# A spectral layer followed by a feed-forward layer on one core: three chunks side by side in the first feed-forward pass, a weight conversion in five stages without GpSimd, and batch 1 behind that pass

## The chip, the cores and the metric

The kernel runs on one core of one Trainium2 chip. The metric is the device time of one execution in microseconds (us), and lower is better. TensorE is called PE here, VectorE DVE, ScalarE ACT, GpSimd POOL; SP is the engine that issues all the transfers.

## The reference

Eight batches of 3008 x 256 numbers go through a spectral layer, and its output, 24064 rows of 256, through a feed-forward layer with 2048 hidden units. The two weights of the feed-forward layer are stored as 64-bit floats.

```python
X = np.fft.rfft(x, axis=1)
Yr = Xr @ w_r - Xi @ w_i + b_r
Yi = Xr @ w_i + Xi @ w_r + b_i
Yr = np.sign(Yr) * np.maximum(np.abs(Yr) - lam, 0.0)     # Yi likewise, lam = 0.01
y = np.fft.irfft(Yr + 1j * Yi, n=3008, axis=1)
h = y.reshape(24064, 256) @ w_in
out = (h - np.tanh(h)) @ w_out
```

## The kernel before

The Fourier transform of length 3008 = 64 x 47 is made of matrix products in stages, with the intermediate results kept in device memory. `Forward(b, ch)` makes the 47-point stage of batch b for four pairs of rows (eight `ch` for each batch, two halves `q` in each) and stores it to `a`. `Spectrum(b, jp)` (twelve `jp` for each batch; `WholeSpectrum` for batch 0) loads `at` from `a`, makes the 64-point stage (`dft`), the product with the complex weights (`cross`, `shared`), the thresholding (`shrink`, `join`) and the first stage back (`inverse`, `put`), and stores it to `z`. A `Chunk` is 5 pairs, 470 columns: it loads `zin` from `z` (which waits for all twelve stores of the batch), makes the last stage back (`time`) into `yh` and `yl`, the rounded part and the rest of the number, and then for each of the 16 blocks f of hidden units `up(f)` (6 matmuls into `h`; ACT makes the tanh `th`, DVE the difference `g`, ACT its rounded copy `gh`, DVE the rest `gl`) and `down(f)` (6 matmuls into two accumulators `o`). A matmul in this way is three products of rounded and rest parts.

`order` lists the pairs (chunk, f) of all FFN work. At step g the program issues `up` for step g + 2 and `down` for step g. The first pass takes chunks 0 and 1 in turn (32 steps), after that one chunk follows the other, 16 steps each. Transforms of later batches and the weight conversion are put into numbered slots, which `run(g)` issues at step g.

The head of the program, up to the first `time` of chunks 0 and 1, stands under `manual_schedule`: there each engine takes its instructions in the order in which the code is written. Everything behind it is ordered by the compiling layer's scheduler. Each engine works through its own list in order and waits at the first instruction whose inputs are not there. `idle(n)` issues n matmuls of 512 columns whose result nobody reads.

The weights come as 16 raw blocks of 512 KB, four for each quarter of f; `split_f64` turns one into two F32R tiles with integer operations: 6 on DVE, 3 on ACT and 2 on POOL for each block. Six blocks are converted in the head, ten in the first pass. Two chunks of the forward stage of batch 1 are made in the head (`following`), the other six from slot 8 on, the spectrum of batch 1 from slot 31 on, one unit every 4 steps.

## Time and profile before

| | before |
|---|---|
| median of 3 runs | 2720.86 us (2720.68 to 2721.68) |
| the profiled execution | 2719.45 us |
| its span, first to last instruction | 2717.2 us |
| PE busy | 2682.9 us, 99% of the span |
| DVE, ACT, POOL busy | 1746.0, 1388.9, 48.9 us |
| mean granted clock of PE | 0.996 of full speed |

The span is 2.3 us shorter than the execution that it was taken from, and that execution 1.4 us shorter than the median of the runs. Matmuls are pipelined, so two that follow each other overlap in the profile, and the time from one start to the next says more than the duration of one.

### The profile page before, as it was taken

What the parts mean: (1) busy time and instruction counts of PE and PEld (TensorE: products, weight loads), DVE (VectorE), ACT (ScalarE), POOL (GpSimd) and SP (SyncE); (2) the same over time, 40 slices, a digit from 0 to 9 for tenths busy, and PEclk for the clock granted to TensorE, in tenths of its full rate; (3) what the DMA queues carried; (4) which work ended last, traced back from release to release, by engine and by line L of the source; (5) the groups of instructions that cost most, each with busy time, mean ns of one, the idle gap of its engine ahead of it and who ended that gap; (6) DMA issues with size and microseconds to landing.
All of it is one profiled execution on the core that took longest, in us unless ns stands there. A gap on an engine that the chain in (4) does not pass through costs nothing.

```text
span 2717.2 us, 36997 instructions
## 1 busy us (share of the span) xinstructions
PE 2682.9 (99%) x14159; PEld 2390.0 (88%) x14159; DVE 1746.0 (64%) x3056; ACT 1388.9 (51%) x2606; POOL 48.9 (2%) x39
## 2 busy tenths in 40 slices
PE   8889999999999999999999999999999999999999
PEld 6679888999889998899988999899988999998989
DVE  5796775766656666567665666656675667655555
ACT  5664455444554445545455454645446544444445
POOL 1230000000000000000000000000000000000000
PEclk9899999999999999999999999999999999999999
DMA  6442114111141113211023110311104111100000
GB/s 198 146 127 65 47 52 125 42 49 36 36 115 49 38 36 96 75 46 49 28 58 101 38 53 30 105 58 48 49 23 123 46 42 40 35 22 22 20 19 17
DMA packets 105137, 163.49 MB, mean 60 GB/s; under 512 B 7488, under 2 KB 70976, under 8 KB 104864
## 3 DMA queue, kind: packets, MB, share of 16 engines
...
q14 instruction: 66, 0.54, 0.1%
...
## 4 chain that ended last, share of the span: by engine, by line
PE 92%; DVE 5%; ACT 2%; issue 1%; DMA 1%; POOL 0%; SPq 0%; DVEq 0%; ACTq 0%
PE o L437 36%; PE h L416 36%; PE ps_v L286 4%; PE ps_i L403 4%; PE ps_f L266 3%; PE ps_t L286 2%; DVE y L311 1%; PE ps_f L217 1%; PE ps_f L219 1%; PE ps_f L218 1%; PE ps_i L322 1%; PE ps_i L323 1%; PE ps_i L321 1%; DVE g L421 1%; DVE gl L425 0%
## 5 line engine op out<-in xcount | busy, mean ns | idle before, releaser
L421 DVE TENSOR_TENSOR g<-h,th 128x470 f32<-128x470 f32 (+1 forms) x832 | 532.0, 639 | 554.6 <-ACT th L419 547.0
L419 ACT ACTIVATE th<-h 128x470 f32<-128x470 f32 (+1 forms) x832 | 464.1, 558 | 765.9 <-PE h L416 765.6
L425 DVE TENSOR_TENSOR gl<-g,gh 128x470 fp32r<-128x470 f32 (+1 forms) x832 | 534.5, 643 | 289.3 <-ACT gh L423 204.8
L423 ACT CAST gh<-g 128x470 fp32r<-128x470 f32 (+1 forms) x832 | 483.1, 581 | 392.6 <-DVE g L421 384.3
L437 PE MATMUL o<-gh,wout_l 128*128 128x470 f32 (+1 forms) x1664 | 632.8, 380 | 0.1
L437 PE MATMUL o<-gl,wout_h 128*128 128x470 f32 (+1 forms) x1664 | 617.1, 371 | 3.1 <-DVE gl L425 3.1
L437 PE MATMUL o<-gh,wout_h 128*128 128x470 f32 (+1 forms) x1664 | 616.1, 370 | 0.0
L416 PE MATMUL h<-yh,win_l 128*128 128x470 f32 (+1 forms) x1664 | 481.0, 370 | 4.1 <-DVE g L421 4.1
L416 PE MATMUL h<-yl,win_h 128*128 128x470 f32 (+1 forms) x1664 | 481.1, 370 | 1.6 <-DVE yl L408 1.5
L416 PE MATMUL h<-yh,win_h 128*128 128x470 f32 (+1 forms) x1664 | 480.1, 369 | 0.0
L437 PEld LDWEIGHTS o<-gl,wout_h 128*128 128x128 f32 x1664 | 313.1, 188 | 44.8 <-DVE gl L425 6.2
L416 PEld LDWEIGHTS h<-yh,win_l 128*128 128x128 f32 x1664 | 310.6, 188 | 41.9 <-DVE g L421 5.1
L437 PEld LDWEIGHTS o<-gh,wout_l 128*128 128x128 f32 x1664 | 313.4, 188 | 35.2 <-DVE ot L446 1.3
L416 PEld LDWEIGHTS h<-yl,win_h 128*128 128x128 f32 x1664 | 310.7, 188 | 37.7 <-DVE yl L408 2.2
L437 PEld LDWEIGHTS o<-gh,wout_h 128*128 128x128 f32 x1664 | 313.9, 189 | 32.2
L416 PEld LDWEIGHTS h<-yh,win_h 128*128 128x128 f32 x1664 | 310.7, 188 | 35.6
L311 DVE TENSOR_TENSOR y<-tb,ps_v 64x256 f32<-64x256 f32 x384 | 160.0, 417 | 9.7 <-ACT tb L358 5.7
L403 PEld LDWEIGHTS ps_i<-i,zin 96*128 96x128 f32 x1024 | 126.2, 192 | 3.0
L403 PE MATMUL ps_i<-i,zin 96*128 96x94 f32 x1024 | 127.7, 272 | 0.0
L91 DVE TENSOR_TENSOR x_l<-xt,x_h 94x512 fp32r<-94x512 f32 x128 | 87.8, 694 | 54.1 <-ACT x_h L90 54.1
L266 PEld LDWEIGHTS ps_f<-f,at 128*128 128x128 f32 x768 | 99.5, 189 | 9.3 <-issue 4.3
L266 PE MATMUL ps_f<-f,at 128*128 128x128 f32 x768 | 101.1, 273 | 1.8 <-DMA at<-a 1.8
...
## 6 DMA issues: line engine op xcount, KB each, us to landing
...
w_raw<-in_moe_w_in SPq DMA_DIRECT2D x8, 512.0 KB, 4.2
w_raw<-in_moe_w_out SPq DMA_DIRECT2D x8, 512.0 KB, 4.4
```

The source lines that it names most:

```text
L91: rest.tensor_tensor(out=lo, in0=src, in1=hi.bitcast(F32), op=ALU.subtract)
L217: nc.tensor.matmul(pv, f1h, xl, start=True, stop=False)
L266: nc.tensor.matmul(pv[:, t, jj], self.at[:, jj, t * P:(t + 1) * P], rhs, start=True, stop=True)
L286: nc.tensor.matmul(dst, lhs[:, t], rhs[:, t, :], start=n == 0, stop=n == 5)
L311: nc.vector.tensor_tensor(out=y[ri * 64:(ri + 1) * 64, jj, :], in0=common(jj, ri), in1=self.vv[jj * 64:(jj + 1) * 64, ri * D:(ri + 1) * D] ...
L403: nc.tensor.matmul(ps[:, k * 94:(k + 1) * 94], self.zt[:, k, t * P:(t + 1) * P], i2t[:, p * 94:(p + 1) * 94], start=True, stop=True,)
L416: nc.tensor.matmul(h[:, :n], lhs[:, t, f * P:(f + 1) * P], rhs[:, t, :n], start=k == 0, stop=k == 5)
L419: nc.scalar.activation(out=th[:, :n], in_=h[:, :n], func=AF.Tanh)
L421: nc.vector.tensor_tensor(out=g[:, :n], in0=h[:, :n], in1=th[:, :n], op=ALU.subtract)
L423: nc.scalar.copy(out=gh[:, :n], in_=g[:, :n])
L425: nc.vector.tensor_tensor(out=gl[:, :n], in0=g[:, :n], in1=gh[:, :n].bitcast(F32), op=ALU.subtract)
L437: nc.tensor.matmul(self.o[t][:, :n], lhs[:, f, t * P:(t + 1) * P], rhs[:, :n], start=f == 0 and k == 0, stop=f == NF - 1 and k == 2,)
```

## The change

The program of each raw block is now five stages: `fields` (2 operations on DVE), `mantissa` (1 on ACT, 1 on DVE), `scale` (3 on DVE), `high` (1 on ACT), `low_part` (1 on DVE); POOL does none. `some(n)` issues the next n stages, taken in turn from two blocks that are under way. Six blocks are loaded in the loop of the head, two behind the loads of the chunks, eight in the first pass. The first pass runs chunks 0, 1 and 2 side by side (48 steps, chunk 0 two blocks f ahead), chunks 0 and 1 accumulate in the four `ps_f` banks and chunk 2 in the two `ps_o` banks, and steps up to 39 stand under `manual_schedule` too. `up` ends with `gh`; `gl` is made by `rest`, behind what `between` issues. The two chunks of batch 1's forward stage leave the head; all eight stand at slots 46 to 53, both halves of one in a slot, and its spectrum from slot 59 on, one unit every 2 steps. `idle` of 12 before the first `time` becomes 26, and one of 8 stands before the last `inverse` of batch 0. The three splits of the linear weights move from units 3 to 5 of the loop to units 0 to 2, and the loads of `at` run two units ahead instead of three.

```diff
-        def exponent():
+        def fields():
             nc.vector.tensor_scalar(out=s, in0=top, scalar1=20, scalar2=0x7FF, op0=ALU.logical_shift_right, op1=ALU.bitwise_and)
-            nc.vector.tensor_scalar(out=s, in0=s, scalar1=-896.0, scalar2=0.0, op0=ALU.add, op1=ALU.max)
+            nc.vector.tensor_scalar(out=m, in0=top, scalar1=0xFFFFF, scalar2=0x100000, op0=ALU.bitwise_and, op1=ALU.bitwise_or)
 
         def mantissa():
-            nc.vector.tensor_scalar(out=m, in0=top, scalar1=0xFFFFF, scalar2=0x100000, op0=ALU.bitwise_and, op1=ALU.bitwise_or)
-            nc.vector.tensor_scalar(out=s, in0=s, scalar1=254.0, scalar2=2.0**23, op0=ALU.min, op1=ALU.mult)
-            nc.scalar.mul(out=w, in_=low, mul=2.0**-32)
-            nc.scalar.copy(out=m.bitcast(F32), in_=m)
-            nc.gpsimd.tensor_tensor(out=w, in0=w, in1=m.bitcast(F32), op=ALU.add)
+            nc.scalar.activation(out=s.bitcast(F32), in_=s, func=AF.Relu, bias=rebias)
+            nc.vector.scalar_tensor_tensor(out=w, in0=low, scalar=2.0**-32, in1=m, op0=ALU.mult, op1=ALU.add)
 
         def scale():
+            nc.vector.tensor_scalar(out=s, in0=s.bitcast(F32), scalar1=254.0, scalar2=2.0**23, op0=ALU.min, op1=ALU.mult)
             nc.vector.scalar_tensor_tensor(out=s, in0=top, scalar=0x80000000, in1=s, op0=ALU.bitwise_and, op1=ALU.bitwise_or)
-
-        def parts():
             nc.vector.scalar_tensor_tensor(out=w, in0=w, scalar=2.0**-20, in1=s.bitcast(F32), op0=ALU.mult, op1=ALU.mult)
+
+        def high():
             nc.scalar.copy(out=hi_out, in_=w)
-            nc.gpsimd.tensor_tensor(out=lo_out, in0=w, in1=hi_out.bitcast(F32), op=ALU.subtract)
-
-        return exponent, mantissa, scale, parts
-
-    def ffn_weights(part, k):
-        for op in split_f64(part, k, load_f64(part, k, load, "zin")):
-            op()
-
-    def convert(units):
-        units = [split_f64(*u) for u in units]
-        ops = []
-        for i in range(len(units) + 1):
-            ops += units[i][:3] if i < len(units) else ()
-            ops += units[i - 1][3:] if i else ()
-        return ops
+
+        def low_part():
+            nc.vector.tensor_tensor(out=lo_out, in0=w, in1=hi_out.bitcast(F32), op=ALU.subtract)
+
+        return [fields, mantissa, scale, high, low_part]
...
+    FIRST = 3
...
-                self.yh = work.tile([P, 2, 512], F32R, name="yh", tag="yh")
-                self.yl = work.tile([P, 2, 512], F32R, name="yl", tag="yl")
+                tags = ("st", "st") if self.c == FIRST - 1 else ("yh", "yl")
+                self.yh, self.yl = (work.tile([P, 2, 512], F32R, name=m, tag=g) for m, g in zip(("yh", "yl"), tags))
...
             gh = ffn.tile([P, CT], F32R, name="gh", tag="g_h")
             nc.scalar.copy(out=gh[:, :n], in_=g[:, :n])
+            return g, gh
+
+        def rest(self, g, gh):
+            n = self.n
...
-                if self.c == 1:
+                if self.c < FIRST - 1:
...
-    order = [(g % 2, g // 2) for g in range(2 * NF)]
-    order += [(c, f) for c in range(2, NCH) for f in range(NF)]
+    SKEW = 2
+    order = [(0, f) for f in range(SKEW)]
+    for f in range(NF):
+        order += [(c, f) for c in range(1, FIRST)] + [(0, f + SKEW)] * (f + SKEW < NF)
+    order += [(c, f) for c in range(FIRST, NCH) for f in range(NF)]
...
-        where = {0: "yh", 1: "yl", 2: "yh", 3: "yl", 7: "yh", 8: "yl"}
-        raws, ops = [], []
...
+        homes = [(work, "yh"), (work, "yl")] * 2 + [(load, "xt")] * 6 + [(load, "zin")] * 2 + [(load, "xt")] * 2 + [(load, "zin")] * 2
+        streams = [[], []]
+        raw_count = 0
+        turn = 0
+
+        def load_raw(n):
+            nonlocal raw_count
+            for _ in range(n):
+                k = raw_count
+                raw_count += 1
+                raw = load_f64(k // 4, k % 4, *homes[k])
+                streams[k % 2].append((k, raw))
+
+        pending = [[], []]
+
+        def some(n):
+            nonlocal turn
+            for _ in range(n):
+                for side in (turn, 1 - turn):
+                    if not pending[side] and streams[side]:
+                        k, raw = streams[side].pop(0)
+                        pending[side] = split_f64(k // 4, k % 4, raw)
+                    if pending[side]:
+                        pending[side].pop(0)()
+                        turn = 1 - side
+                        break
...
+        raw_at = {0: 2, 4: 1, 5: 1, 9: 1, 10: 1}
+        some_at = (0, 2, 2, 1, 1, 1, 1, 2, 1, 2, 1, 2, 1)
+        for u in units[:2]:
+            u.load()
...
+            some(some_at[i])
+            if i == NU:
+                unit(i - 1).common()
...
+            if i < 3:
+                lin.append(split(whole_lin[i], f"w{i + 1}"))
...
-        u9, u10, u11 = units[-3:]
-        for q in range(2):
-            following[0].split(q)
+        u10, u11 = units[-2:]
         u10.inverse()
-        u11.common()
         u11.shrink()
-        for q in range(2):
-            following[0].dft(q)
         u10.put(u10.pz)
+        some(1)
         u11.join()
+        idle(8)
         u11.inverse()
         u11.put(u11.pz)
-        for c in range(2):
+        for c in range(FIRST):
             chunks[c].load()
-        for q in range(2):
-            following[0].keep(q)
-        for q in range(2):
-            following[1].split(q)
-        for op in ops[:6]:
-            op()
-        for q in range(2):
-            following[1].dft(q)
-            following[1].keep(q)
-        idle(12)
+        load_raw(2)
+        some(6)
+        idle(26)
         for c in range(2):
             for t in range(2):
                 chunks[c].time(t)
-            for op in ops[6 + c:7 + c]:
-                op()
-
-    for i in range(2):
-        put(2 * i - 2, ffn_weights, 1, 2 + i)
-    for i in range(8):
-        put(1 + 8 * i // 3, ffn_weights, 2 + i // 4, i % 4)
-    plan_forward(1, 8, 2, 3, LOOK)
-    plan_spectrum(1, 31, 4, 7, 2)
+        some(5)
+
+        ready, half = {}, {}
+
+        def step(g, between):
+            if g + AHEAD < len(order):
+                c, f = order[g + AHEAD]
+                half[g + AHEAD] = chunks[c].up(f)
+            between()
+            if g + AHEAD in half:
+                c, f = order[g + AHEAD]
+                ready[g + AHEAD] = chunks[c].rest(*half.pop(g + AHEAD))
+            if g < 0:
+                return
+            c, f = order[g]
+            chunks[c].down(f, *ready.pop(g))
+            if f == NF - 1:
+                chunks[c].store()
+
+        HELD = 40
+        raw_slots = (-1, 2, 6, 9, 13, 16, 19, 22)
+
+        def early(g):
+            if g == -1:
+                for t in range(2):
+                    chunks[2].time(t)
+            if g in raw_slots:
+                load_raw(1)
+            some(1 + (g % 5 in (0, 2)))
+
+        for g in range(-AHEAD, HELD):
+            step(g, lambda: early(g))
+    plan_forward(1, 46, 1, 3)
+    plan_spectrum(1, 59, 2, 3, 1)
...
-    for c in range(2, NCH):
+    for c in range(FIRST, NCH):
         at = NF * (c - 1)
-        put(at + {2: 9, 6: 6}.get(c, 2), chunks[c].load)
+        put(at + {FIRST: 8, 6: 7}.get(c, 2), chunks[c].load)
         for t in range(2):
-            put(at + (13 if c == 2 else 8 + 2 * t + (2 if c == 6 else 0)), chunks[c].time, t)
-    ready = {}
-    for g in range(-AHEAD, len(order)):
-        if g + AHEAD < len(order):
-            c, f = order[g + AHEAD]
-            ready[g + AHEAD] = chunks[c].up(f)
-        run(g)
-        if g < 0:
-            continue
-        c, f = order[g]
-        chunks[c].down(f, *ready.pop(g))
-        if f == NF - 1:
-            chunks[c].store()
+            put(at + (12 if c == FIRST else 10 + t if c == 6 else 8 + 2 * t), chunks[c].time, t)
...
+    for g in range(HELD, len(order)):
+        step(g, lambda: run(g))```

**DVE at the start of the first pass.** Before, from the last `yl` of chunk 0 on (`w_s`, `w_m`, `w_f` belong to the conversion):

```order
L161 TENSOR_SCALAR w_s<-w_raw 128x512
L165 TENSOR_SCALAR w_m<-w_raw 128x512
L162 TENSOR_SCALAR w_s<-w_s 128x512
L408 TENSOR_TENSOR yl<-ps_i_1015,yh 128x470
L408 TENSOR_TENSOR yl<-ps_i_1023,yh 128x470
L175 SCALAR_TENSOR_TENSOR w_f<-w_f,w_s 128x512
L421 TENSOR_TENSOR g<-h,th 128x470
L166 TENSOR_SCALAR w_s<-w_s 128x512
L421 TENSOR_TENSOR g<-h,th 128x470
L425 TENSOR_TENSOR gl<-g,gh 128x470
```

The same place after the change (L398 is `yl`, L411 `g`, L419 `gl`, L169 to L171 `scale`, L177 `low_part`):

```order
L398 TENSOR_TENSOR yl<-ps_i_990,yh 128x470
L169 TENSOR_SCALAR w_s<-w_s 128x512
L170 SCALAR_TENSOR_TENSOR w_s<-w_raw,w_s 128x512
L171 SCALAR_TENSOR_TENSOR w_f<-w_f,w_s 128x512
L169 TENSOR_SCALAR w_s<-w_s 128x512
L170 SCALAR_TENSOR_TENSOR w_s<-w_raw,w_s 128x512
L171 SCALAR_TENSOR_TENSOR w_f<-w_f,w_s 128x512
L177 TENSOR_TENSOR win_l<-w_f,win_h 128x512
L411 TENSOR_TENSOR g<-h,th 128x470
L177 TENSOR_TENSOR win_l<-w_f,win_h 128x512
L419 TENSOR_TENSOR gl<-g,gh 128x470
```

Seven operations of the conversion now stand between the last `yl` of chunk 1 and the first `g`, and conversion work stands between `g` and `gl` instead of behind `gl`.

**PE at the end of the head.** Before, from the inverse of unit 9 of batch 0 on (L217 to L219 are batch 1's forward stage, the last `ps_i` is unit 11):

```order
L373 MATMUL ps_i_892<-mn,i_f 128x512
L373 MATMUL ps_i_905<-mn,i_f 128x512
L217 MATMUL ps_f_918<-x_0_0_l,f_h 96x512
L218 MATMUL ps_f_918<-x_0_0_h,f_l 96x512
L219 MATMUL ps_f_918<-x_0_0_h,f_h 96x512
L217 MATMUL ps_f_922<-x_0_1_l,f_h 96x512
L218 MATMUL ps_f_922<-x_0_1_h,f_l 96x512
L219 MATMUL ps_f_922<-x_0_1_h,f_h 96x512
L373 MATMUL ps_i_930<-mn,i_f 128x512
L217 MATMUL ps_f_967<-x_1_0_l,f_h 96x512
```

After:

```order
L361 MATMUL ps_i_874<-mn,i_f 128x512
L361 MATMUL ps_i_879<-mn,i_f 128x512
L493 MATMUL idle<-warm 128x512 x8
L361 MATMUL ps_i_904<-mn,i_f 128x512
L493 MATMUL idle<-warm 128x512 x26
L393 MATMUL ps_i_964<-i_382,zin 128x94 x5
```

The forward stage of batch 1 is gone from here, and idle matmuls stand in its place on both sides of the last inverse.

**PE in the spectrum of batch 1.** Before, one FFN step with its filling (L286 is `cross` and `shared`, L416 `up`, L437 `down`):

```order
L416 MATMUL h<-yl,win_h 128x470 x2
L286 MATMUL ps_v<-w_h,xl 128x256 x2
L286 MATMUL ps_v<-w_l,xh 128x256 x2
L286 MATMUL ps_v<-w_h,xh 128x256 x2
L437 MATMUL o_2099<-gh,wout_l 128x470
```

After (L406 is `up`, L309 to L311 `inverse`, L274 `cross` and `shared`, L431 `down`):

```order
L406 MATMUL h<-yl,win_h 128x470 x2
L309 MATMUL ps_i_3205<-z_3_l,i_h 128x512
L310 MATMUL ps_i_3205<-z_3_h,i_l 128x512
L311 MATMUL ps_i_3205<-z_3_h,i_h 128x512
L274 MATMUL ps_t_3212<-w_h,s_4_l 128x256 x2
L274 MATMUL ps_t_3212<-w_l,s_4_h 128x256 x2
L274 MATMUL ps_t_3212<-w_h,s_4_h 128x256 x2
L274 MATMUL ps_v<-w_h,xl 128x256 x2
L274 MATMUL ps_v<-w_l,xh 128x256 x2
L274 MATMUL ps_v<-w_h,xh 128x256 x2
L431 MATMUL o_2934<-gh,wout_l 128x470
```

One step now carries work of three units (an inverse, a shared product, a cross product) between `up` and `down`.

## Rows read from the trace of the kernel before

**Rows 1.** The page, part 1: busy time, share of the span, instructions.

```profile
PE 2682.9 (99%) x14159; PEld 2390.0 (88%) x14159; DVE 1746.0 (64%) x3056; ACT 1388.9 (51%) x2606; POOL 48.9 (2%) x39
```

**Rows 2.** Windows by stage: length, busy of each engine (x), PEclk, DMA share, GB/s.

```profile
34.50:87.30 52.80, 49.03 (x234) 38.30 (x235) 36.40 (x75) 30.31 (x57) 11.69 (x9) 1.00 0.54 170
87.30:115.50 28.20, 20.07 (x67) 12.61 (x66) 18.35 (x37) 15.84 (x31) 4.11 (x3) 0.82 0.44 132
115.50:195.00 79.50, 69.71 (x321) 56.41 (x320) 73.81 (x117) 51.44 (x96) 31.44 (x23) 0.98 0.41 121
195.00:440.00 245.00, 243.97 (x1310) 214.27 (x1309) 170.19 (x303) 131.67 (x251) 0.20 (x1) 1.00 0.26 79
440.00:2717.00 2277.00, 2272.45 (x12142) 2049.81 (x12140) 1430.21 (x2495) 1142.64 (x2143) 0.00 (x0) 1.00 0.17 50
```

**Rows 3.** Timeline of PE in the head: start, duration, instruction, idle time before it.

```profile
60.23 0.46 PE L348 MATMUL ps_v<-brow,ones 33*128 33x512 f32 x1 [0.60 <-DVE y L311]
...
67.27 0.47 PE L348 MATMUL ps_v<-brow,ones 33*128 33x512 f32 x1 [2.04 <-DVE y L311]
...
73.18 0.46 PE L348 MATMUL ps_v<-brow,ones 33*128 33x512 f32 x1 [0.90 <-DVE y L311]
...
82.24 1.05 PE L266 MATMUL ps_f<-f,at 128*128 128x128 f32 x8
...
87.35 1.05 PE L266 MATMUL ps_f<-f,at 128*128 128x128 f32 x8
```

**Rows 4.** Timeline from unit 11's thresholding to the first chunk.

```profile
100.66 1.72 DVE L311 TENSOR_TENSOR y<-tb,ps_v 64x256 f32<-64x256 f32 x4
...
103.77 0.69 DVE L369 TENSOR_TENSOR mn<-up,mn 128x512 f32<-128x512 f32 x1 [1.40 <-ACT mn L365]
...
104.52 2.08 PE L373 MATMUL ps_i<-mn,i_f 128*128 128x512 f32 x2 [2.75 <-DVE mn L369]
...
115.54 4.60 PE L403 MATMUL ps_i<-i,zin 96*128 96x94 f32 x40
```

**Rows 5.** Waits of PE in 115.5 to 195: total us, times, longest.

```profile
PE h L416 <- DVE g L421: 4.1, 4, 1.5
PE o L437 <- DVE gl L425: 3.1, 5, 1.4
PE h L416 <- DVE yl L408: 1.5, 1, 1.5
PE ps_f L217 <- DVE x_l L91: 1.0, 1, 1.0
```

**Rows 6.** Timeline of DVE, pairs that follow each other without a wait.

```profile
112.55 0.68 DVE L172 SCALAR_TENSOR_TENSOR w_s<-w_raw,w_s 128x512 uint32<-128x512 uint32 x1
...
113.15 0.42 DVE L161 TENSOR_SCALAR w_s<-w_raw 128x512 uint32<-128x512 uint32 x1
...
122.41 0.42 DVE L165 TENSOR_SCALAR w_m<-w_raw 128x512 uint32<-128x512 uint32 x1
122.75 0.42 DVE L162 TENSOR_SCALAR w_s<-w_s 128x512 uint32<-128x512 uint32 x1
...
132.54 0.63 DVE L421 TENSOR_TENSOR g<-h,th 128x470 f32<-128x470 f32 x1
...
133.10 0.63 DVE L425 TENSOR_TENSOR gl<-g,gh 128x470 fp32r<-128x470 f32 x1
```

**Rows 7.** Groups of DVE in 115.5 to 195: busy, mean ns, idle before.

```profile
L425 DVE TENSOR_TENSOR gl<-g,gh 128x470 fp32r<-128x470 f32 x21 | 16.3, 778 | 1.2 <-ACT gh L423 1.1
L421 DVE TENSOR_TENSOR g<-h,th 128x470 f32<-128x470 f32 x21 | 13.3, 635 | 0.0
```

**Rows 8.** The first of these groups in 204 to 420.

```profile
L425 DVE TENSOR_TENSOR gl<-g,gh 128x470 fp32r<-128x470 f32 x60 | 38.8, 647 | 19.9 <-ACT gh L423 17.7 <-PE o L437 1.3
```

**Rows 9.** Timeline of PE, the starts of two `up` with one `down` between.

```profile
243.63 0.58 PE L416 MATMUL h<-yh,win_l 128*128 128x470 f32 x2
...
246.15 0.58 PE L416 MATMUL h<-yh,win_l 128*128 128x470 f32 x2
```

**Rows 10.** Window of one spectrum unit of batch 1, columns as in rows 2.

```profile
300.49:314.76 14.27, 14.12 (x79) 12.54 (x78) 10.37 (x19) 6.78 (x14) 0.00 (x0) 1.00 0.12 38
```

**Rows 11.** The page, part 6: DMA issues, KB each, us to landing.

```profile
w_raw<-in_moe_w_in SPq DMA_DIRECT2D x8, 512.0 KB, 4.2
```

More of the change, by code (lines that the diff above doesn't have):

```diff
@@ L443, in store @@
             n = self.n
-            ot = work.tile([P, 2, 512], F32, name="ot", tag="ot", bufs=1)
+            if self.c == FIRST - 1:
+                ot = load.tile([P, 2, 512], F32, name="ot", tag="zin")
+            else:
+                ot = work.tile([P, 2, 512], F32, name="ot", tag="ot", bufs=1)
             nc.scalar.copy(out=ot[:, 0, :n], in_=self.o[0][:, :n])
@@ L497, in spectral_ffn @@
         nc.vector.memset(below, -LAM)
+        rebias = const.tile([P, 1], F32, name="rebias")
+        nc.vector.memset(rebias, -896.0)
         f1h, f1l = split(load_whole(f1, [94, 96], "f1", tag="tmp", bufs=4), "f1")
@@ L541, in spectral_ffn @@
                 unit(i).dft()
+            if unit(i - 1):
+                unit(i - 1).cross()
             if unit(i - 2):
@@ L545, in spectral_ffn @@
                 unit(i).sum()
-            if unit(i - 1):
-                unit(i - 1).cross()
+            some(some_at[i])
+            if i == NU:
+                unit(i - 1).common()
             if unit(i - 2):
```

28 lines of the change are left out of this document (6 added, 22 removed).

## The prediction

> **What bounds the kernel now.** I read the busy shares first: PE is busy for 99% of the span and DVE for 64% [rows 1]. So time can only come out of places where PE waits or runs idle matmuls, and the windows by stage say where these are. From 440 us on PE is busy 2272.45 of 2277 us [rows 2], and none of that can be won. What lies open is in the first 200 us: 3.8 us in the loop over the units of batch 0 (49.03 busy of 52.8), 8.1 us in the stretch to the first chunk (20.07 of 28.2, at a granted clock of 0.82, and 12 of its matmuls idle ones), and 9.8 us in the first FFN pass (69.71 of 79.5). The timeline and the waits then name the partner. In the loop PE waits three times for DVE's `y`, 0.60, 2.04 and 0.90 us [rows 3]. In the pass it waits 9.7 us in all, every time for DVE: 4.1 and 1.5 for `g` and `yl`, 3.1 for `gl`, 1.0 for `x_l` [rows 5]. There DVE is busy 73.81 of 79.5 us [rows 2]. The first 200 us are DVE's, the rest is PE's.
>
> **The conversion.** Its price on DVE has to be taken from starts, since operations overlap: a two-input one of 0.68 us lets the next start 0.60 us later, a one-input one of 0.42 us after 0.34, `g` after 0.56 [rows 6]. A block took 4 one-input and 2 two-input operations, 4 x 0.34 + 2 x 0.60 = 2.6 us; now it takes 3 and 4, 3 x 0.34 + 4 x 0.60 = 3.4 us. So DVE gets 0.8 us more for each block. Against that stands that POOL falls silent. While it worked, `gl` took 778 ns, and 647 ns in the stretch behind [rows 7, 8]; `g`, which reads PSUM, took 635 ns, so it was not stretched. ACT goes from three operations to two, and it was busy 51.44 of 79.5 us [rows 2], so it stays out of the sum; if it were full, each operation less would be worth some 0.6 us.
>
> The Trainium skill says what separates the two (GPSIMD Engine Reference, section 1, Specifications): GpSimd shares its SBUF interfaces with VectorE, and contends with instructions in a two-port mode or with two SBUF inputs. By that the stretching ends with POOL's work, and 3.4 us for a block holds; the stretched `gl` beside the unstretched `g` agrees [rows 7]. If the stretching had another cause, the block would keep it, which is a rival below.
>
> **The loop of the head.** Units follow each other in 5.11 us where nothing waits [rows 3]. DVE's part of a unit is `y` 1.72, `sf` some 0.4 and the join 0.6 [rows 4, 6], with two stages at most beside it: 2.7 + 2 x 0.7 = 4.1 us. Only one unit carries two `scale` stages (2 x (0.34 + 0.60 + 0.60) = 3.1 us, 5.8 in all), and it is the last. So the three waits go: -3.5 us. The floor is nothing (the waits return elsewhere). Two raw blocks stand ahead of the third `at` in SP's queue; with 4.2 us for a block [rows 11] it comes about when PE gets there, so I count nothing and keep 1 us for the range. The constant `rebias` is one memset of 128 x 1.
>
> **From the last unit to the first chunk.** Before, this took 115.54 - 87.35 = 28.2 us, of which the last inverse ended at 104.52 + 2.08 = 106.6; from there to the first chunk's matmul (copy, store of `z`, load of `zin`) went 8.9 us [rows 3, 4]. That last part is data's way and stays. The part ahead is a chain on DVE: 2.0 us until `sf`, two `scale` 3.1, a join 0.6, then twice a thresholding with its join, 103.77 + 0.69 - 100.66 = 3.8 us each [rows 4], and the inverse 1.0: 14.3 us instead of 19.3. So the first chunk's matmul comes 28.2 - 23.2 = 5.0 us earlier. The idle matmuls fill what PE waits anyway: 26 of them at 0.23 us are 6 us of the 8.9. They would cost only if `zin` came within 6 us. But two chunks of batch 1's forward stage, four halves of three matmuls, stood in this wait for nothing, and are paid later: twelve matmuls of 512 columns. A 470-column one costs (246.15 - 243.63) / 12 = 0.21 us [rows 9], so 12 x 0.23 = +2.7 us. Net -2.3.
>
> **The first pass.** A step (`up` and `down`) takes PE 2.52 us [rows 9]. DVE's share of it: `g` and `gl` 1.12, and 1.4 stages of 3.4 / 5 us, 0.95; 2.1 us in all. So DVE keeps up once the pass runs, and the place that waits is its start. From the order: four `yl` are done 5.6 us after the first chunk's matmul, then come two `scale` and a `low_part` (3.7 us) ahead of the first `g`, so `gl` of the first block and with it the first `down` come at about 11 us, the second waits for chunk 2's `yl` and for two `fields`, the third for `gl` behind two more stages, and the two `scale` at step 2 push one `gl` to 23.7 us. I add up PE's work to the point where DVE is level, 27 us: three chunks' `time` at 2.3 us (half of the 4.6 that two took [rows 4]) and 14 halves of a step at 1.26 make 24.5. So 2.5 us are lost. For the handover to chunk 3, where three chunks are stored within five steps, I add 1.5. Against 9.7 us of waits and 0.02 x 79.5 = 1.6 us lost to the lower clock [rows 2, 5]: 4.0 - 11.3 = -7.3 us. Bounds: -10 if DVE hides all of it, 0 if the waits stay as they are. What queues behind a late DVE operation here is `g`, and behind that the next `up`, which needs the bank that `g` frees.
>
> The third chunk lives in buffers that lie free then (`st`, `zin`); nothing waits for them before slot 46. Raw blocks 6 and 7 wait on SP until `scale` of 4 and 5 frees their buffers, some 7 us into the pass; they land 4.2 us later [rows 11], and `fields` is due at 14. Had they 7 us to go, `gl` of the second block would wait behind them.
>
> **Batch 1.** Its spectrum had four steps for a unit and has two. One unit costs PE 14.27 - 4 x 2.52 = 4.2 us (with what `time` adds on average) and DVE 10.37 - 4 x 1.12 = 5.9 [rows 6, 9, 10]. Two steps with a unit are then 9.2 us on PE and 8.1 on DVE. With the parts of batch 2's forward stage in the later half, two for each pair of steps, it is 10.6 and 9.3. PE stays the longer one, so I count nothing for the twelve units (bounds: 0 and 1 us for each). In the forward stage two halves a step are 3.9 us on PE, and on ACT four operations of some 0.6 beside `th` and `gh`, 3.6 us: nothing, at most 2 us. What I do count is chunk 6, which needs the first pairs of batch 1: its load stands one slot behind the last inverse, the way from inverse to chunk is the 8.9 us of above, and the order shows about that much PE work between, and one `down` without an `up` behind it. +1.5 us, from 0 to 4.
>
> **The sum.** -3.5 - 2.3 - 7.3 + 1.5 = -11.6 us on the profiled execution's 2719.45, which is 2707.9; the median of the runs stands 1.4 higher, so 2709.3, said as 2709.5 us. A change of 0.2%, 5.4 us, is about what a measurement can tell here.
>
> **The rivals.** *DVE binds batch 1 (slower).* At two steps a unit DVE has 1.1 us of slack in 9.2, and every unit has waits in it that run across engines (`s_h`, then the shared product, then `y`, then the rounding of `z`). If 3 us of such waits lie open in each, the period is 11.1 instead of 9.2, and 12 units cost 23 us: 2732. It decides at 1 us a unit, where the whole gain is gone. For it speaks that in the old order DVE was 73% busy in such a unit [rows 10] and had steps to spare; against it that a late DVE no longer waits for PE, so the waits shrink as it gets late.
>
> *The pass stays DVE's (no change).* If operations run in full length (0.42, 0.68) and stretched by `gl`'s 0.13 us, a block costs 4.0 + 0.9 and a step 1.4 + 1.4 = 2.8 us, over PE's 2.52. Then 33 steps lose 9 us, and the start about 3 more: 2709.5 + 12 = 2721. For it speaks 73.81 of 79.5 in the old pass [rows 2]; against it the starts in rows 6, and that `g` took no longer beside POOL [rows 7].
>
> *The head's gain is not given on (no change, or just faster).* If `zin` lands no earlier, since the loads of the raw blocks and of `i2` keep the transfers busy (DMA share 0.44 [rows 2]), the 5 us of the transition and the loop's 3.5 fall away: 2718.
>
> **How the numbers follow.** Forecast 0.66, with 2703 to 2716 as its own range; DVE binding batch 1 0.12 (one part in six of it costs so little that the time stays within 0.2%); the pass staying DVE's 0.14; the head's gain lost 0.08. Faster by more than 0.2%, below 2715.4: 0.68. Within 0.2%: 0.22. Slower: 0.10. The range 2701 to 2722 takes in the bounds (-10 for the pass, nothing for chunk 6) and the two middle cases.
>
> **What would show it.** In the profile after: no wait of PE for `y` in the loop; the first chunk's matmul at about 107 us instead of 115.54; waits of PE for `g`, `gl` and `yl` in the first 30 us behind it and then none; `gl` at 650 ns there, the one-input operations at 0.42 us; a pass of 48 steps in some 132 us. PE waits for `xl`, `z_l` or PSUM banks between slots 59 and 86, each about 1 us or more, would make the forecast wrong, and so would a DVE that is busy for over 95% of the pass.

## The result and the profile after

The change makes the kernel slower: 2728.48 us, median of 10 runs (2725.47 to 2733.6), against 2720.86 us of the kernel before, median of 10 runs. The ratio is 1.0028, with a 95% interval of 1.0018 to 1.0038. The forecast was 2709.5 us, with 2701 to 2722 as its range. The profiled execution of the changed kernel took 2728.08 us.

The page's busy times and the windows by stage, columns as in [rows 2], of the kernel after:

```profile
PE 2708.4 (99%) x14181; PEld 2401.1 (88%) x14181; DVE 1745.7 (64%) x3075; ACT 1387.9 (51%) x2590; POOL 1.5 (0%) x5
...
34.16:84.58 50.42, 50.42 (x234) 39.55 (x235) 37.29 (x79) 30.02 (x54) 0.00 (x0) 0.97 0.57 174
84.58:108.45 23.87, 20.55 (x78) 14.35 (x76) 14.53 (x30) 10.38 (x19) 0.00 (x0) 0.93 0.29 92
108.45:140.00 31.55, 28.59 (x153) 25.43 (x154) 23.78 (x42) 14.64 (x28) 0.00 (x0) 0.95 0.40 113
140.00:195.00 55.00, 55.00 (x260) 48.55 (x259) 48.92 (x89) 32.13 (x59) 0.00 (x0) 1.00 0.23 65
195.00:440.00 245.00, 243.89 (x1300) 213.51 (x1299) 180.32 (x320) 138.80 (x268) 0.00 (x0) 1.00 0.32 93
440.00:2726.00 2286.00, 2282.36 (x12072) 2041.29 (x12071) 1423.77 (x2485) 1144.94 (x2133) 0.00 (x0) 1.00 0.17 50
```

The first stages did what was forecast. In the loop of the head PE is busy for all of its 50.42 us, the way to the first chunk takes 23.87 us instead of 28.2 [rows 2], and from 140 to 195 us PE never waits. And yet PE as a whole is busy for 25.5 us more than before (2708.4 against 2682.9 in [rows 1]), with 22 matmuls more, all idle ones. That is the row to stop at: work that nobody added.

PE's timeline of the kernel after, from the last unit's `at` (84.58) over the last inverse (100.28) to the first chunk's matmul (108.45), the first and the 49th `up`, and two `up` of neighbouring steps near the end:

```profile
84.58 1.05 PE L254 MATMUL ps_f<-f,at 128*128 128x128 f32 x8
...
100.28 1.02 PE L361 MATMUL ps_i<-mn,i_f 128*128 128x512 f32 x2
108.45 4.67 PE L393 MATMUL ps_i<-i,zin 96*128 96x94 f32 x40 [1.21 <-DMA zin<-z]
112.91 0.67 PE L406 MATMUL h<-yh,win_l 128*128 128x470 f32 x2
...
244.16 0.59 PE L406 MATMUL h<-yh,win_l 128*128 128x470 f32 x2
...
2503.95 0.59 PE L406 MATMUL h<-yh,win_l 128*128 128x470 f32 x2
2506.51 0.59 PE L406 MATMUL h<-yh,win_l 128*128 128x470 f32 x2
```

The last two rows show the loss. A step of 12 matmuls takes 2506.51 - 2503.95 = 2.56 us; before it took 2.52 [rows 9]. Nothing waits there and the granted clock is full; each 470-column matmul simply starts 3 ns later after the one ahead. The 256 pairs of rows make 52 chunks, 50 of 5 pairs and 2 of 3, and at 16 steps each that is 832 steps.

Waits of PE of the kernel after from 108 to 240 us, besides the 1.21 for `zin` above: total us, times, longest.

```profile
PE h L406 <- DVE g L411: 1.9, 1, 1.9
PE o L431 <- ACT gh L413: 1.1, 1, 1.1
PE o L431 <- DVE gl L419: 1.1, 1, 1.1
```

### The profile page after: what moved, and what is told of

Same layout as the page of the kernel before. It is cut to its first block, busy times and chain, and to the rows that moved or that the text cites. A ratio compares the mean times of both kernels' runs of the same rounds, so it can differ in the third digit from the quotient of the medians.

```text
span 2726.3 us, 36980 instructions
## 1 busy us (share of the span) xinstructions
PE 2708.4 (99%) x14181; PEld 2401.1 (88%) x14181; DVE 1745.7 (64%) x3075; ACT 1387.9 (51%) x2590; POOL 1.5 (0%) x5
## 3 DMA queue, kind: packets, MB, share of 16 engines
q1 hardware_dynamic: 104960, 161.13, 19.9%
## 4 chain that ended last, share of the span: by engine, by line
PE 97%; DVE 1%; DMA 1%; ACT 0%; issue 0%; SPq 0%; DVEq 0%; ACTq 0%
PE o L431 38%; PE h L406 38%; PE ps_v L274 4%; PE ps_i L393 4%; PE ps_f L254 3%; PE ps_t L274 2%; PE ps_f L205 1%; PE ps_f L206 1%; PE ps_f L207 1%; PE ps_v L342 1%; PE ps_i L309 1%; PE ps_i L310 1%; PE ps_i L311 1%; PE ps_i L361 0%; PE ps_t L342 0%; DVE g L411 0%
## 5 line engine op out<-in xcount | busy, mean ns | idle before, releaser
L411 DVE TENSOR_TENSOR g<-h,th 128x470 f32<-128x470 f32 (+1 forms) x832 | 531.9, 639 | 556.2 <-ACT th L409 552.1
L419 DVE TENSOR_TENSOR gl<-g,gh 128x470 fp32r<-128x470 f32 (+1 forms) x832 | 531.7, 639 | 292.3 <-ACT gh L413 202.3
L413 ACT CAST gh<-g 128x470 fp32r<-128x470 f32 (+1 forms) x832 | 483.4, 581 | 404.7 <-DVE g L411 393.7
L431 PE MATMUL o<-gh,wout_l 128*128 128x470 f32 (+1 forms) x1664 | 632.6, 380 | 1.1 <-ACT gh L413 1.1
L431 PE MATMUL o<-gl,wout_h 128*128 128x470 f32 (+1 forms) x1664 | 620.7, 373 | 1.1 <-DVE gl L419 1.1
L431 PE MATMUL o<-gh,wout_h 128*128 128x470 f32 (+1 forms) x1664 | 619.3, 372 | 0.0
L406 PE MATMUL h<-yh,win_l 128*128 128x470 f32 (+1 forms) x1664 | 485.0, 372 | 1.9 <-DVE g L411 1.9
L406 PE MATMUL h<-yl,win_h 128*128 128x470 f32 (+1 forms) x1664 | 485.8, 373 | 0.0
L406 PE MATMUL h<-yh,win_h 128*128 128x470 f32 (+1 forms) x1664 | 485.2, 373 | 0.0
L431 PEld LDWEIGHTS o<-gl,wout_h 128*128 128x128 f32 x1664 | 313.2, 188 | 41.6 <-DVE gl L419 1.5
L406 PEld LDWEIGHTS h<-yh,win_l 128*128 128x128 f32 x1664 | 311.5, 188 | 43.0 <-DVE g L411 2.1
L406 PEld LDWEIGHTS h<-yl,win_h 128*128 128x128 f32 x1664 | 311.8, 188 | 40.5
L406 PEld LDWEIGHTS h<-yh,win_h 128*128 128x128 f32 x1664 | 311.5, 188 | 39.8
L431 PEld LDWEIGHTS o<-gh,wout_l 128*128 128x128 f32 x1664 | 313.9, 189 | 36.9 <-ACT gh L413 1.6
L431 PEld LDWEIGHTS o<-gh,wout_h 128*128 128x128 f32 x1664 | 313.7, 189 | 34.5
L393 PEld LDWEIGHTS ps_i<-i,zin 96*128 96x128 f32 x1024 | 126.1, 192 | 5.1 <-issue 1.6
L393 PE MATMUL ps_i<-i,zin 96*128 96x94 f32 x1024 | 127.8, 272 | 1.2 <-DMA zin<-z 1.2
L91 DVE TENSOR_TENSOR x_l<-xt,x_h 94x512 fp32r<-94x512 f32 x128 | 86.8, 686 | 50.8 <-ACT x_h L90 49.5
L254 PEld LDWEIGHTS ps_f<-f,at 128*128 128x128 f32 x768 | 101.2, 191 | 10.2 <-issue 4.4
L254 PE MATMUL ps_f<-f,at 128*128 128x128 f32 x768 | 102.7, 276 | 1.9 <-DMA at<-a 1.9
## 6 DMA issues: line engine op xcount, KB each, us to landing
w_raw<-in_moe_w_in SPq DMA_DIRECT2D x8, 512.0 KB, 6.3
w_raw<-in_moe_w_out SPq DMA_DIRECT2D x8, 512.0 KB, 4.2
```

The costliest lines, as they stand in the source:

```text
L91: rest.tensor_tensor(out=lo, in0=src, in1=hi.bitcast(F32), op=ALU.subtract)
L254: nc.tensor.matmul(pv[:, t, jj], self.at[:, jj, t * P:(t + 1) * P], rhs, start=True, stop=True)
L393: nc.tensor.matmul(ps[:, k * 94:(k + 1) * 94], self.zt[:, k, t * P:(t + 1) * P], i2t[:, p * 94:(p + 1) * 94], start=True, stop=True,)
L406: nc.tensor.matmul(h[:, :n], lhs[:, t, f * P:(f + 1) * P], rhs[:, t, :n], start=k == 0, stop=k == 5)
L411: nc.vector.tensor_tensor(out=g[:, :n], in0=h[:, :n], in1=th[:, :n], op=ALU.subtract)
L413: nc.scalar.copy(out=gh[:, :n], in_=g[:, :n])
```

## The experiments

The theory that I formed from this: the new constant is guilty, not the new order. `rebias` holds 4 bytes in each partition, but takes 32, and it is allocated behind the FFN weights and ahead of nearly everything else. So all tiles behind it move by 32 bytes against the weights. The addresses in the compiled programs (byte in the partition, first buffer of each; remainder by 256 in brackets):

```
          before         after
win_h     16512 (128)    16512 (128)
wout_l    65664 (128)    65664 (128)
below     82048 (128)    82048 (128)
rebias    -              82080 (160)
yh        145056 (160)   145088 (192)
gl        204448 (160)   204480 (192)
gh        210592 (160)   210624 (192)
```

The rivals are the new order of the steps or the new stream of instructions. Three kernels part them.

**e1_carve: the constant without its 32 bytes.**

```diff
-        below = const.tile([P, 1], F32, name="below")
-        rebias = const.tile([P, 1], F32, name="rebias")
+        pair = const.tile([P, 2], F32, name="below")
+        below, rebias = pair[:, 0:1], pair[:, 1:2]
```

> The changed kernel with `rebias` as the second column of `below`'s tile, so that every tile behind it in SBUF lies where it lay before the change; nothing else differs. Theory A (32 bytes of offset: with `rebias` as a tile of its own yh, yl, gh and gl start at multiples of 64 bytes, as the weights do, and a 470-column matmul then takes 214 to 215 ns instead of 210 to 211): the steady spacing goes back to 210 to 211 ns and the time falls by some 33 us, to 2690 to 2702 us, 0.988 to 0.993 of the kernel before. Theory B (the new order of the steps or the new instruction stream slows TensorE everywhere): 2728 us, ratio 1.003, spacing 214 ns.

Measured: 2701.34 us, ratio 0.9929 (0.9914 to 0.9944). Its timeline of PE, with the last two inverses of the head, the first chunk's matmul and two `up` near the end:

```profile
94.96 1.10 PE L361 MATMUL ps_i<-mn,i_f 128*128 128x512 f32 x2 [2.11 <-DVE mn L357]
...
98.76 1.13 PE L361 MATMUL ps_i<-mn,i_f 128*128 128x512 f32 x2 [0.84 <-DVE mn L357]
...
107.18 4.67 PE L393 MATMUL ps_i<-i,zin 96*128 96x94 f32 x40 [1.36 <-DMA zin<-z]
...
2509.19 0.58 PE L406 MATMUL h<-yh,win_l 128*128 128x470 f32 x2
2511.71 0.58 PE L406 MATMUL h<-yh,win_l 128*128 128x470 f32 x2
```

The step is back at 2.52 us, PE is busy for 2680.0 us by the page, and the same instructions in the same order are 27 us faster. It is faster than the kernel before by 0.7%.

**e2_before_pad: the kernel before with the 32 bytes and nothing else.**

```diff
         nc.vector.memset(below, -LAM)
+        rebias = const.tile([P, 1], F32, name="rebias")
+        nc.vector.memset(rebias, -896.0)
```

> The kernel before with the tile `rebias` of the change added behind `below` and a memset of it, read by nobody; every tile behind it moves by 32 bytes, and no other instruction differs. Theory A (the offset): the spacing of the 470-column matmuls goes from 210 to 211 up to 214 to 215 ns over the whole FFN, some 10000 matmuls by 3.3 ns, and the time to 2748 to 2756 us, ratio 1.010 to 1.013. Theory B (the order or the stream): 2721 us, ratio 1.000.

Measured: 2744.47 us, ratio 1.0090 (1.0073 to 1.0107). Two neighbouring `up` in its timeline of PE:

```profile
2531.10 0.59 PE L416 MATMUL h<-yh,win_l 128*128 128x470 f32 x2
2533.66 0.59 PE L416 MATMUL h<-yh,win_l 128*128 128x470 f32 x2
```

The kernel before gets the step of 2.56 us from a tile that nobody reads. The direction and the step are as expected; the time stays below the expected 2748, because 0.04 us for each of 832 steps, 33 us, is too much for the whole: over all steps, those with other work in them too, the loss is nearer 0.03 (below).

**e3_late_between: the old order of a step from step 40 on.**

```diff
-            between()
+            if g < HELD:
+                between()
             if g + AHEAD in half:
                 ...
+            if g >= HELD:
+                between()
```

> The changed kernel, with the other work of a step (Forward, Spectrum, time) put behind the step's `gl` instead of between `g` and `gl` from step 40 on, which is the order of the kernel before; the 32 bytes of `rebias` stay. Theory A (the offset): the spacing stays 214 to 215 ns and the time within 4 us of the changed kernel's, 2725 to 2732 us, ratio 1.001 to 1.004. Theory B (the order of the steps): the spacing goes back to 210 to 211 ns and the time to 2690 to 2702 us, ratio 0.988 to 0.993.

Measured: 2727.73 us, ratio 1.0024 (1.0013 to 1.0034), as the changed kernel. Two neighbouring `up` in its timeline of PE:

```profile
2534.20 0.59 PE L406 MATMUL h<-yh,win_l 128*128 128x470 f32 x2
2536.76 0.59 PE L406 MATMUL h<-yh,win_l 128*128 128x470 f32 x2
```

The step stays at 2.56 us. The order of the steps isn't it.

**e4_pad64 and e5_pad96: other offsets.** A tile behind `rebias`, of 32 bytes in the first, and of 64 bytes, `[P, 16]`, in the second.

```diff
+        pad = const.tile([P, 8], F32, name="pad")
+        nc.vector.memset(pad, 0.0)
```

> The changed kernel with a tile of 32 bytes behind `rebias`: yh, yl, gh and gl then start 64 bytes further than in the kernel before, at 96 over a multiple of 128 (before: at 32 over, changed kernel: at 64 over). Theory A64 (a moving operand is slow where it starts on a multiple of 64 bytes): spacing 210, time 2698 to 2705 us, ratio 0.992 to 0.994. Theory A128 (a moving operand is slow where its 1880 bytes touch 16 lines of 128 bytes instead of 15, which happens at 64 and at 96 over a multiple of 128): spacing 213 to 215 ns, time 2725 to 2732 us, ratio 1.002 to 1.004.

> The changed kernel with a tile of 64 bytes behind `rebias`: yh, yl, gh and gl start 96 bytes further than before, on a multiple of 128. Theory A64 (slow on a multiple of 64): spacing 213 to 215 ns, time 2725 to 2732 us, ratio 1.002 to 1.004. Theory A128 (slow where 16 lines of 128 bytes are touched; here it is 15): spacing 210 ns or less, time 2695 to 2705 us, ratio 0.990 to 0.994.

Measured: 2729.24 us, ratio 1.0036 (1.0023 to 1.0049), and 2728.73, 1.0031 (1.0018 to 1.0044). Two neighbouring `up` of each, in this order:

```profile
2535.27 0.59 PE L406 MATMUL h<-yh,win_l 128*128 128x470 f32 x2
2537.83 0.59 PE L406 MATMUL h<-yh,win_l 128*128 128x470 f32 x2
```

```profile
2533.44 0.59 PE L406 MATMUL h<-yh,win_l 128*128 128x470 f32 x2
2536.00 0.59 PE L406 MATMUL h<-yh,win_l 128*128 128x470 f32 x2
```

Both take 2.56 us for a step, so both of my simple rules fall, multiples of 64 bytes as well as lines of 128. Of the four offsets, only that of the kernel before is fast.

**e6_ffn_pad: 32 bytes for the FFN's own tiles only**, `rebias` as in e1_carve.

```diff
+        pad = ffn.tile([P, 8], F32, name="pad", tag="pad", bufs=1)
+        nc.vector.memset(pad, 0.0)
         warm = ffn.tile([P, 512], F32R, name="warm", tag="g_l")
```

> The changed kernel with `rebias` in the tile of `below` and a tile of 32 bytes at the start of the pool of the FFN: gh, gl, th and g lie on multiples of 64 as in the changed kernel, yh and yl where they lay before. Theory A (each matmul's own moving operand decides): matmuls into `h` (rhs yh, yl) 210 ns apart, matmuls into `o` (rhs gh, gl) 213 to 215, time halfway, 2712 to 2718 us, ratio 0.997 to 0.999. Rival (what ACT and DVE read and write, th, g and the halves, slows the reads of every matmul): both kinds 213 to 215 ns apart, 2725 to 2732 us; or, if only yh and yl matter, both 210 and 2701 us.

Measured: 2720.54 us, ratio 1.0004 (0.9995 to 1.0014). One step in its timeline of PE (start of `up`, of `down`, of the next `up`):

```profile
2533.27 0.59 PE L406 MATMUL h<-yh,win_l 128*128 128x470 f32 x2
...
2534.54 0.38 PE L431 MATMUL o<-gh,wout_l 128*128 128x470 f32 x1
...
2535.82 0.59 PE L406 MATMUL h<-yh,win_l 128*128 128x470 f32 x2
```

The six matmuls of `down`, whose operands moved, take 1.28 us, and those of `up`, whose operands didn't, 1.27 (1.26 each at a step of 2.52). By the starts in the trace, over 290 steps without other work in them, only the first of `up`, right behind `down`, is slow (216 ns to the next start); the other five stay at 210 on average. I had expected half the loss and saw some 19 of 27 us. So a matmul's spacing does not follow from its own moving operand alone.

**e8_sweep and e9_sweep_all32: 42 starts in one run**, `rebias` as in e1_carve. Each chunk's operands start at a column of their own; `gl` is cut as `gh`. In the second kernel a tile of 32 bytes ahead of all others moves the weights too.

```diff
+            self.oy, self.og = (5 * self.c) % 42, (11 * self.c + 20) % 42
...
+                    work.tile([P, 2, 512], F32R, name=m, tag=g)[:, :, self.oy:self.oy + n] for m, g in zip(("yh", "yl"), tags)
...
-            gh = ffn.tile([P, CT], F32R, name="gh", tag="g_h")
+            gh = ffn.tile([P, 512], F32R, name="gh", tag="g_h")[:, self.og:self.og + n]
```

> The changed kernel with `rebias` in the tile of `below`, and in every chunk c the moving operands start at a column of their own in the tiles: yh and yl at column 5c mod 42, gh and gl at column 11c + 20 mod 42, 4 bytes each, so that one run reads the spacing of the 470-column matmuls at 42 starts from 32 to 196 bytes over a multiple of 128. Rows to read: the mean spacing of the matmuls into `h` and into `o` by chunk. Theory A, by its own place alone: the same spacing of either kind at the same start, 210 ns at column 0 and 213 to 215 at columns 8, 16 and 24 (the three offsets run so far), and 210 again at column 32, 128 bytes on, if what counts repeats by 128. Rival (the place against other tiles, not its own): column 32 gives 213 to 215 or anything between. The whole lies between 2701 and 2732 us.

> The same run over 42 starts, with a tile of 32 bytes ahead of all others, so that the weights too lie 32 bytes further (at 32 over a multiple of 128 instead of on one). Theory A-own (the moving operand's own start counts): the fast columns are 8 lower than in the run before, so that column 24 (now 32 over a multiple of 128) is fast and column 0 (64 over) is slow, 213 to 215 ns. Theory A-between (what counts is where the moving operand lies against the weights, 32 bytes after a multiple of 128 of theirs): the fast columns are the same ones as in the run before, column 0 at 210 ns.

One execution each: 2730.51 and 2731.68 us. PE's timeline in chunks 40, 46 and 49 of e8_sweep, then in chunks 46 and 49 of e9_sweep_all32:

```profile
2228.39 0.60 PE L409 MATMUL h<-yh,win_l 128*128 128x470 f32 x2
...
2229.70 0.37 PE L434 MATMUL o<-gh,wout_l 128*128 128x470 f32 x1
...
2508.70 0.60 PE L409 MATMUL h<-yh,win_l 128*128 128x470 f32 x2
...
2509.98 0.38 PE L434 MATMUL o<-gh,wout_l 128*128 128x470 f32 x1
...
2511.30 0.60 PE L409 MATMUL h<-yh,win_l 128*128 128x470 f32 x2
...
2639.31 0.58 PE L409 MATMUL h<-yh,win_l 128*128 128x470 f32 x2
2641.85 0.58 PE L409 MATMUL h<-yh,win_l 128*128 128x470 f32 x2
```

```profile
2509.88 0.59 PE L410 MATMUL h<-yh,win_l 128*128 128x470 f32 x2
2512.48 0.59 PE L410 MATMUL h<-yh,win_l 128*128 128x470 f32 x2
...
2640.50 0.58 PE L410 MATMUL h<-yh,win_l 128*128 128x470 f32 x2
2643.04 0.58 PE L410 MATMUL h<-yh,win_l 128*128 128x470 f32 x2
```

Chunk 46 (columns 20 and 22) has steps of 2.60 us, chunk 49 (columns 35 and 13) of 2.54, in both runs, although every operand lies 32 bytes further in the second. By the starts in both traces this holds for every chunk from 2 to 49: in steps without other work the length goes from 2539 to 2600 ns with the chunk, and the two runs differ by at most 2 ns. So distances count and not addresses. In chunk 40 yh and yl start at column 32, 128 bytes further than in the fast kernel, and the six matmuls of `up` take 2229.70 - 2228.39 = 1.31 us, 218 ns each: unless the place of `gh` and `gl`, column 40 there, makes this, the pattern has no period of 128 bytes. I found no simple rule over the 42 starts.

**e10_all32 and e13_weights32: which distance**, both with `rebias` in the tile of `below`. The first puts a tile of 32 bytes ahead of the weights, so that everything moves; the second puts that tile itself there instead, so that the weights alone move.

```diff
+    pad = const.tile([P, 8], F32, name="pad")
     win_h = const.tile([P, 2, FF], F32R, name="win_h")
```

```diff
+    pair = const.tile([P, 2], F32, name="below")
     win_h = const.tile([P, 2, FF], F32R, name="win_h")
...
-        pair = const.tile([P, 2], F32, name="below")
```

> The changed kernel with `rebias` in the tile of `below` and a tile of 32 bytes ahead of the FFN weights: weights, yh, yl, gh and gl all lie 32 bytes further than before, so the moving operands start where the changed kernel has them, and their distances from the weights and from each other are those of the kernel before. Theory A-between (the place of the moving operand against the weights and the other tiles counts): spacing 210 ns, 2698 to 2705 us, ratio 0.992 to 0.994, as with `rebias` in the tile of `below` alone. Theory A-own (its own start counts): spacing 213 to 215 ns, 2725 to 2732 us, ratio 1.002 to 1.004.

> The changed kernel with `rebias` in the tile of `below`, and that tile ahead of the FFN weights instead of behind them: the weights alone lie 32 bytes further, on the same residue of 256 bytes as the moving operands; every other tile lies where it lay in the kernel before. Theory A-weights (what counts is the distance between a matmul's moving operand and its weights): spacing 213 to 216 ns, 2725 to 2735 us, ratio 1.002 to 1.006. Theory A-others (what counts is the distance between the moving operands of successive matmuls, or to what ACT and DVE read and write, all unchanged here): spacing 210 ns, 2698 to 2705 us, ratio 0.992 to 0.994.

Measured: e10_all32 2704.1 us, ratio 0.9936 (0.9918 to 0.9954); e13_weights32 2727.06 us, ratio 1.0034 (1.0020 to 1.0049). Two neighbouring `up` of each, in this order:

```profile
2514.85 0.58 PE L407 MATMUL h<-yh,win_l 128*128 128x470 f32 x2
2517.37 0.58 PE L407 MATMUL h<-yh,win_l 128*128 128x470 f32 x2
```

```profile
2504.98 0.59 PE L407 MATMUL h<-yh,win_l 128*128 128x470 f32 x2
2507.54 0.59 PE L407 MATMUL h<-yh,win_l 128*128 128x470 f32 x2
```

With the operands where the changed kernel has them, but the weights moved along, a step takes 2.52 us; with the operands where the kernel before has them, but the weights 32 bytes further, it takes 2.56. The distance between weights and moving operands decides; in e8_sweep these operands moved alone, with `th` and `g` in place, and the step changed with them.

**e7_two: two chunks side by side.** `FIRST = 2`, the conversion packed into 28 steps, batch 1 16 steps earlier, `rebias` as in e1_carve.

```diff
-    FIRST = 3
+    FIRST = 2
-            some(1 + (g % 5 in (0, 2)))
+            some(2 + (g % 5 in (0, 2)))
```

> The changed kernel with `rebias` in the tile of `below`, and two chunks instead of three in the first pass: conversion, head and the steps' order stay as changed, the conversion is packed into 28 steps instead of 40, and batch 1's Forward and Spectrum start 16 steps earlier. Theory C (the third chunk is what takes the waits of the pass, since DVE has the same conversion to do in 32 steps instead of 48): 5 to 11 us over the kernel with three chunks, 2706 to 2712 us, ratio 0.994 to 0.997, with waits of TensorE for gl, gh or yl in the first 60 us of the FFN. Rival (the head's earlier start and the loss of GpSimd's stages gave it): within 3 us of three chunks, 2698 to 2704 us, ratio 0.992 to 0.994.

Measured: 2713.4 us, ratio 0.9979 (0.9970 to 0.9989), 12 us over three chunks. Waits of PE from 106 to 210 us:

```profile
PE o L431 <- DVE gl L419: 6.6, 8, 2.2
PE h L406 <- DVE g L411: 4.6, 2, 4.1
```

The third chunk is what covers the conversion; without it PE waits 11.2 us for DVE, close to the 9.7 of the old pass [rows 5].

**e11_pool: GpSimd back in the conversion**, `rebias` as in e1_carve.

```diff
-            nc.vector.scalar_tensor_tensor(out=w, in0=low, scalar=2.0**-32, in1=m, op0=ALU.mult, op1=ALU.add)
+            nc.scalar.mul(out=w, in_=low, mul=2.0**-32)
+            nc.scalar.copy(out=m.bitcast(F32), in_=m)
+            nc.gpsimd.tensor_tensor(out=w, in0=w, in1=m.bitcast(F32), op=ALU.add)
...
-            nc.vector.tensor_tensor(out=lo_out, in0=w, in1=hi_out.bitcast(F32), op=ALU.subtract)
+            nc.gpsimd.tensor_tensor(out=lo_out, in0=w, in1=hi_out.bitcast(F32), op=ALU.subtract)
```

> The changed kernel with `rebias` in the tile of `below`, and with GpSimd back in the conversion: the sum of the mantissa's parts (after two copies on ACT) and `low_part` run on GpSimd, as in the kernel before; the five stages and their places stay. Theory of the prediction (GpSimd stretches `gl` by some 0.13 us while it works, DVE is given 1.2 us for each block, and the pass is TensorE's but for its start): `gl` at 750 to 790 ns in the first pass, time within 3 us of the kernel without GpSimd, 2698 to 2705 us, ratio 0.992 to 0.994. Rival (it was GpSimd that kept the first pass and the head waiting, by its slow stages in the chain of a block): 5 us or more above it, 2706 to 2712 us, ratio 0.994 to 0.997.

Measured: 2719.52 us, ratio 1.0000 (0.9990 to 1.0009). Its group of `gl` in 108 to 240 us, the longest of its waits of PE in 115 to 235, its window with the first chunk's matmuls and their row in the timeline:

```profile
L421 DVE TENSOR_TENSOR gl<-g,gh 128x470 fp32r<-128x470 f32 x40 | 29.2, 729 | 12.4 <-ACT gh L415 12.4
...
PE o L433 <- DVE gl L421: 8.3, 9, 2.5
...
110.00:116.00 6.00, 6.00 (x29) 5.94 (x29) 1.95 (x3) 1.69 (x4) 0.00 (x0) 0.50 0.29 82
...
108.32 7.29 PE L395 MATMUL ps_i<-i,zin 96*128 96x94 f32 x40 [1.20 <-DMA zin<-z]
```

My theory fails here: with GpSimd in the conversion the kernel is 18 us slower than e1_carve, and not up to 3, although DVE has less to do. `gl` is stretched (729 ns on average, against 647 in [rows 8]), PE waits 8.3 us for it, and PE's clock is granted at half, the lower of its two levels, for the first chunks' matmuls, which take 7.29 us instead of 4.67. The Trainium skill (GPSIMD Engine Reference, section 1, Specifications) has GpSimd contend with instructions of two SBUF inputs, and `gl` is one; the 729 ns agree. ACT also has two operations more for each block here; I didn't run what share of the 18 us is theirs.

**e12_fewidle: 12 idle matmuls instead of 34**, `rebias` as in e1_carve.

```diff
-        idle(8)
...
-        idle(26)
+        idle(12)
```

> The changed kernel with `rebias` in the tile of `below`, without the 8 idle matmuls ahead of the last inverse and with 12 instead of 26 behind it, as many as the kernel before had. Theory of the prediction (they fill what TensorE waits anyway, data's way sets the first chunk's matmul): the first chunk's matmul at the same time within 0.5 us; the granted clock falls in the wait, and with it the first matmuls of the chunks run at the lower of the two levels, which costs 1 to 3 us: 2701 to 2705 us, ratio 0.993 to 0.995. Rival (TensorE works them off when `zin` is there already): the first chunk's matmul 1 to 3 us earlier and the time 2698 to 2701 us, ratio 0.992 to 0.993.

Measured: 2708.68 us, ratio 0.9958 (0.9943 to 0.9974), 7.3 us over e1_carve. Its timeline of PE, from the last but one inverse on, and its window in the first chunks' matmuls:

```profile
96.64 1.10 PE L361 MATMUL ps_i<-mn,i_f 128*128 128x512 f32 x2 [2.11 <-DVE mn L357]
...
100.53 2.04 PE L361 MATMUL ps_i<-mn,i_f 128*128 128x512 f32 x2 [2.79 <-DVE mn L357]
...
109.70 8.82 PE L393 MATMUL ps_i<-i,zin 96*128 96x94 f32 x40 [2.94 <-DMA zin<-z]
...
110.00:116.00 6.00, 6.00 (x30) 6.00 (x29) 1.30 (x2) 1.10 (x2) 0.00 (x0) 0.50 0.14 37
```

After waits of 2.79 and 2.94 us the 40 matmuls run at the lower level and take 8.82 us instead of 4.67, and the two matmuls of the last inverse 2.04 instead of 1.13. Neither expectation holds: the sign is that of the prediction's theory, but it costs more than 1 to 3 us, and the first chunk's matmul too comes 2.5 us later. Of these 2.5 us 1.7 are not the idle matmuls' doing: the last but one inverse, which stands ahead of the first one taken away, is as late already (96.64 against 94.96). The rest is theirs, 0.8 us there and 8.82 - 4.67 = 4.15 us in the 40 matmuls, 5.0 of the 6.1 us between the two profiled executions (2708.39 and 2702.25).

## Why the prediction was wrong

**The step that failed** is in "What bounds the kernel now": "From 440 us on PE is busy 2272.45 of 2277 us, and none of that can be won", and with it "The constant `rebias` is one memset of 128 x 1". I took a saturated engine for a fixed time. PE's busy time is no constant of the work: 32 bytes between the weights and the moving operands made a step 2.56 us instead of 2.52. Over the whole it is 2728.08 - 2702.25 = 25.8 us between the profiled executions of the changed kernel and e1_carve, 0.031 us for each of 832 steps; the kernel before lost 21.3 us by the same tile (spans of 2738.5 and 2717.2). The starts in the traces account for it: between neighbouring 470-column matmuls the mean spacing is 210.75 ns in e1_carve and 213.35 in the changed kernel, and 9600 such matmuls make 25.0 us. That the distance does it is shown by e1, e2, e10 and e13 from four sides. Why certain distances are slow is not: weights are loaded while the matmul ahead still reads its operand (in the changed kernel PEld is busy for 88% of the span and PE for 99%), so a clash of these two reads in SBUF suggests itself, and nothing here measures it.

**The rest held in the main, and was a little undersized.** With the old distances (e1_carve) the profiled execution takes 2702.25 us, 17.2 less than before; the terms made 11.6.
- Loop and way to the first chunk: -3.5 and -5.0 forecast. PE's waits for `y` are gone, units follow in 4.96 us (their `at` matmuls start at 54.81 and 59.77), the last unit's matmul comes at 84.58 instead of 87.35 [rows 3], and the first chunk's at 108.45 (107.18 in e1_carve) instead of 115.54 [rows 4], forecast 107. So -7.1 and -8.4 in the two runs, against -8.5. That the way came out right is luck: the chain up to the end of the last inverse took 100.28 + 1.02 - 84.58 = 16.7 us, forecast 14.3, and data's way behind it 7.2, which I had held fixed at 8.9; the two errors cancel.
- That the idle matmuls are free was right: PE waits for `zin` behind them (1.21 us). What I didn't see is what they give: the work behind the wait ran at the higher clock in e1_carve and at the lower in e12, worth 5.0 us there. They are no guarantee: e11 had all 34 and a wait of 1.20 us, and its 40 matmuls still ran at the lower clock.
- First pass: 48 steps in 131.25 us, forecast 132; the waits are 1.9 us for `g` and 1.1 each for `gh` and `gl`, forecast 2.5 and 1.5.
- Chunk 6: +1.5 forecast, and there is no wait of PE at all from 240 to 450 us in the kernel after.
- What is left, 17.2 - 8.4 + 2.7 for the forward stage paid later = 11.5 us, came behind the first chunk's matmul, where I had 7.3 - 1.5 = 5.8. By the windows, PE's idle time there fell from 9.79 + 1.03 + 4.55 us [rows 2] to 2.96 + 1.11 + 3.64 in the changed kernel, so by 7.7, and to 3.21 + 1.83 + 3.81 in e1_carve, so by 6.5; the lower clock costs as much as before (0.05 x 31.55 against 0.02 x 79.5, 1.6 us each). The other 5.0 us of e1_carve I can't assign; the runs of e1_carve alone lie 2.6 apart (2699.66 to 2702.25).

**The rivals.** DVE doesn't bind batch 1, the pass isn't DVE's, and the head's gain is given on in full. All three spoke of waits, and there are next to none. The price of the conversion on DVE (+0.8 us a block) was wrong: I had read the stretching beside POOL off `gl` and taken a block's operations at their unstretched lengths, but those with one input were stretched too. One of them, in the kernel before (115.5 to 195 us) and after (108 to 240):

```profile
L165 DVE TENSOR_SCALAR w_m<-w_raw 128x512 uint32<-128x512 uint32 x10 | 8.5, 851 | 0.0
```

```profile
L162 DVE TENSOR_SCALAR w_m<-w_raw 128x512 uint32<-128x512 uint32 x10 | 4.2, 420 | 0.0
```

Over the 16 blocks the conversion keeps DVE busy for 63.8 us before and 63.5 after, 4.0 us a block in both. And e11 shows that GpSimd's stages, together with the two ACT operations that they take with them, cost far more than DVE's extra work.
